# Attention, feed-forward and eight experts on one core: the first stage in a written order of single steps, with the first chunk's diagonal terms computed on TensorE

## The chip, the cores and the metric

One core of one Trainium2 chip runs the whole program in one launch. The metric is device microseconds (us) of the execution; each time is given as the median of several runs. The engines are named PE (TensorE), DVE (VectorE), ACT (ScalarE), POOL (GpSimd) and SP (SyncE, which here only issues DMAs).

## The reference

Three stages, each feeding the next, all in float32:

```
# 1. attention with a decaying state: B=2, H=8 heads, S=768 tokens, D=48
for t in range(S):
    cur = outer(u * k[t], v[t])                # the diagonal term, weighted by u
    y[t] = r[t] @ (state + cur)
    state = w[t][:, None] * state + outer(k[t], v[t])
# 2. feed-forward on x = y as 1536 tokens x 384
h = x @ w_in                                   # 384 x 2048
x = (h * clip(h + 3, 0, 6) / 6) @ w_out        # 2048 x 384
# 3. eight experts, all of them for every token, weighted by a Sinkhorn routing P
out = sum over e of P[:, e] * (relu(x @ w1[e]) @ w2[e])     # 384 x 1024 x 384
```

The weights of stage 2 come as 64-bit words and are made into float32 on the chip.

## The kernel before, in words

**Attention in chunks.** The tokens of each batch entry are cut into six chunks of 128; a *block* is one chunk of one of the two batch entries, twelve in all. A block loads its decays `w` (226 KB), `r` and `k` by dimension (`rk`, 448 KB), `v` by token (192 KB), and `r` and `k` once more by token (`rkt`, 384 KB). `prep0` (L149) makes running products of the decays by two scans on DVE, `prep1` multiplies them into `r` and `k`. `scores` (L188) multiplies `k` and `r` on PE and turns `k` over; `masks` (L203) copies the scores out on ACT and cuts the upper triangle on POOL; `outputs` (L215) multiplies by `v`, adds the part of the state, and sums `k` times `v` for the next state; `update` (L237) brings the state on. The diagonal term is apart: `diag0` (L173) multiplies `r`, `k` and `u` by token on POOL, `diag1` (L180) sums each head's 48 numbers on DVE and scales `v` by the sums in eight ACT steps, and `evac` (L232) adds the result to the output. `transposes` and `parts` (L250, L256) turn the block over and split it in a high and a low part, so that the feed-forward can multiply in reduced-width float32 three times (high-high, low-high, high-low) and keep the precision.

**Feed-forward in units.** A *unit* is one of 16 slices of 128 hidden columns for one chunk of both batch entries (256 columns): 96 units. `ff1_up` (L266) is nine matmuls of 128x256, a clamp step and a product (ACT L277, DVE L279), and a split (ACT L282, DVE L283). `ff1_down` (L286) is nine matmuls into two sums in PSUM, and comes two units later. Units are grouped in *cells*: a cell is a chunk and a range of slices, whose sum is copied out or added at its end (L298 to L304). Chunks 0 to 2 go through slices 0 to 5, then 6 to 11, then 12 to 15 (L753); chunks 3 to 5 through all sixteen at once.

**Weights.** Each pair of slices needs a half of `w_in` and a half of `w_out` (768 KB each as 64-bit words): `load_half` (L51) issues the load from SP into one of three buffers, `split_half` (L61) takes three DVE steps (L69 to L71), one ACT step and one DVE subtraction (L113, L114). There are 16 such halves.

**What sets the order.** Each engine and each DMA queue works off its own instructions in order, and waits at the head of its queue. The first block of code is written in an order by hand (L806 to L814), then units, attention stages and conversions are put at unit numbers (`at`, L761 to L800). That order is only a priority: up to the second unit of the experts a planner, which has its own costs for instructions, decides the order on each engine and queue. From there on (L871) the written order holds as it is.

Of the kernel before, what the change touches and what calls it, by code (L numbers as in the profile page):

```python
# [18 lines left out]
DM = H * D  # L19
# [23 lines left out]

class Kernel:
# [16 lines left out]
    def split_half(self, i, n, eng, after=None):  # L61
        if after is not None:
            with self.tc.issue_after(after.ins):
                return self.split_half(i, n, eng)
        nc = self.nc
        st = self.staged.pop((i, n)).rearrange("p (x t) -> p x t", t=2)
        low, high = st[:, :, 0], st[:, :, 1]
        x = self.tmp.tile([128, KT * CH], U32, tag="x", name="x")
        nc.vector.tensor_scalar(out=x, in0=high, scalar1=3, scalar2=0x3FFFFFF8, op0=ALU.logical_shift_left, op1=ALU.bitwise_and)  # L69
        nc.vector.scalar_tensor_tensor(out=x, in0=high, scalar=0xC0000000, in1=x, op0=ALU.bitwise_and, op1=ALU.bitwise_or)  # L70
        nc.vector.scalar_tensor_tensor(out=x, in0=low, scalar=29, in1=x, op0=ALU.logical_shift_right, op1=ALU.bitwise_or)  # L71
        if self.general:
            self.clamp_exponents(x, high)
        self.parts_of("ab"[n], x.bitcast(F32), (i // NCH, i % NCH, n), eng)
# [29 lines left out]
    def split_chunk(self, i, eng):  # L104
        st = self.staged.pop(i)
        h = KT * CH
        for n in range(2):
            self.parts_of("ab"[n], st[:, n * h:(n + 1) * h], (2 + i // NCH, i % NCH, n), eng)

    def parts_of(self, nm, x, key, eng):  # L110
        hi = self.wp.tile([128, KT * CH], F32R, tag=f"w{nm}h", name=f"w{nm}h")
        lo = self.wp.tile([128, KT * CH], F32R, tag=f"w{nm}l", name=f"w{nm}l")
        self.nc.scalar.activation(hi, x, AF.Copy)  # L113
        eng.tensor_tensor(out=lo, in0=x, in1=hi.bitcast(F32), op=ALU.subtract)  # L114
        self.wt[key] = hi, lo
# [9 lines left out]
    def att_load(self, c, b):  # L125
        nc, att = self.nc, self.att
        src = self.dm[b, c]
        w = att.tile([KR, WCOL], F32, tag="w", name="w")
        nc.sync.dma_start(out=w, in_=src[:, 2 * NP * C:])
        rk = att.tile([KR, 2 * NP * C], F32, tag="rk", name="rk")  # L130
        nc.sync.dma_start(out=rk, in_=src[:, :2 * NP * C])
        v = att.tile([C, DM], F32, tag="v", name="v")
        nc.sync.dma_start(out=v, in_=self.tm[b, c][:, 2 * DM:])
        self.loaded[c, b] = w, rk, v

    def att_load_tokens(self, c, b):
        self.tokens_of = c, b
        self.rkt = self.att.tile([C, 2 * DM], F32, tag="rkt", name="rkt")
        self.nc.sync.dma_start(out=self.rkt, in_=self.tm[b, c][:, :2 * DM])

    def att_stages(self, c, b):
        nc, att = self.nc, self.att
        w, rk, vt = self.loaded.pop((c, b))
        r = rk[:, :NP * C].rearrange("p (i t) -> p i t", i=NP)
        k = rk[:, NP * C:].rearrange("p (i t) -> p i t", i=NP)
        q = {}
        first, last = c == 0, c == NC - 1

        def prep0():  # L149
            wi = w[:, 1:].rearrange("p (i t) -> p i t", i=NP)[:, :, :C]  # L150
# [3 lines left out]
                data1=self.d1e.rearrange("p i t -> p (i t)"), initial=0.0, op0=ALU.mult, op1=ALU.add)  # L154
            rev = lambda x: x[:, ::-1]
            d1 = self.d1f
# [5 lines left out]
            q["f"], q["e"] = f, e  # L162

        def prep1():
            f, e = q["f"], q["e"]
            nc.vector.tensor_tensor(out=r, in0=r, in1=e[:, :, :C], op=ALU.mult)
            nc.vector.tensor_tensor(out=k, in0=k, in1=f[:, :, 1:], op=ALU.mult)
            if not last:
                pt = att.tile([KR, NP, 1], F32, tag="pt", name="pt")
                nc.vector.tensor_copy(pt, e[:, :, C:])  # L170
                q["pt"] = pt

        def diag0():  # L173
            assert self.tokens_of == (c, b)
            rt, kt = self.rkt[:, :DM], self.rkt[:, DM:]
            nc.gpsimd.tensor_tensor(out=rt, in0=rt, in1=kt, op=ALU.mult)
            nc.gpsimd.tensor_tensor(out=rt, in0=rt, in1=self.ubt, op=ALU.mult)
            q["z"] = rt

        def diag1():  # L180
            sd = att.tile([C, H], F32, tag="sd", name="sd")
            nc.vector.tensor_reduce(out=sd, in_=q["z"].rearrange("p (h d) -> p h d", h=H), axis=AX.X, op=ALU.add)
            dv = att.tile([C, DM], F32, tag="dv", name="dv")
            for h in range(H):
                nc.scalar.activation(dv[:, h * D:(h + 1) * D], vt[:, h * D:(h + 1) * D], AF.Copy, scale=sd[:, h:h + 1])  # L185
            q["dv"] = dv

        def scores():  # L188
            early = first and b == 1
            sc = [(self.psg if early else self.psa).tile([C, NP, C], F32, tag="g" if early else "sc", name="sc")  # L190
                  for _ in range(2)]
# [4 lines left out]
            if not last:  # L196
                kp = (self.psx if early else self.psa).tile([C, NP, KR], F32, tag="xa" if early else "m", name="kp")
                for i in range(NP):
                    nc.tensor.transpose(kp[:, i, :], k[:, i, :], self.ident[:KR, :KR])
                q["kp"] = kp  # L200
            q["sc"] = sc

        def masks():  # L203
            a = att.tile([C, 2, NP, C], F32, tag="a", name="a")
            for j in range(2):
                nc.scalar.activation(a[:, j], q["sc"][j], AF.Copy)
                nc.gpsimd.affine_select(out=a[:, j], in_=a[:, j], pattern=[[0, NP], [1, C]], compare_op=ALU.is_gt,
                                        fill=0.0, base=0, channel_multiplier=-1)
            q["a"] = a
            if not last:  # L210
                ks = att.tile([C, NP, KR], F32, tag="ks", name="ks")
                nc.scalar.activation(ks, q["kp"], AF.Copy)
                q["ks"] = ks

        def outputs():  # L215
# [10 lines left out]
            if not last:  # L226
                u = self.psa.tile([KR, NP, 2 * D], F32, tag="m", name="u")
                for i in range(NP):
                    nc.tensor.matmul(u[:, i, :], q["ks"][:, i, :], vt[:, i * 96:(i + 1) * 96], start=True, stop=True)
                q["u"] = u  # L230
# [6 lines left out]
        def update():  # L237
            if last:
                return
            for j in range(2):  # L240
# [3 lines left out]
                else:  # L244
                    nc.vector.tensor_tensor(out=self.state[b][p, :, e], in0=q["u"][p, :, e],
                                            in1=self.state[b][p, :, e], op=ALU.add)
            for i in range(NP):
# [8 lines left out]
        def parts():  # L256
            if b == 0:
                self.x1[c] = tuple(self.x1p.tile([128, KT, NB1], F32R, tag=f"x1{s}", name=f"x1{s}") for s in "hl")
            hi, lo = (t[:, :, b * C:(b + 1) * C] for t in self.x1[c])
            nc.scalar.activation(hi, q["xp"], AF.Copy)  # L260
            nc.vector.tensor_tensor(out=lo, in0=q["xp"], in1=hi.bitcast(F32), op=ALU.subtract)

        return [prep0, prep1, diag0, scores, diag1, masks, outputs, evac, update, transposes, parts]


    def ff1_up(self, c, f, start, stop):  # L266
        nc = self.nc
        ah, al = self.up_parts(f // 8, f % 8)
        xh, xl = self.x1[c]
        ph = self.psg.tile([128, 512], F32, tag="g", name="ph")[:, :NB1]  # L270
        n = 0
        for kt in range(KT):
            for wa, xa in ((ah, xh), (ah, xl), (al, xh)):
                nc.tensor.matmul(ph, wa[:, kt, :], xa[:, kt, :], start=n == 0, stop=n == 3 * KT - 1)  # L274
                n += 1
        t = self.p1.tile([128, NB1], F32, tag="t", name="t")
        nc.scalar.activation(t, ph, AF.Relu, bias=self.three)  # L277
        u = t
        self.last_u = nc.vector.scalar_tensor_tensor(out=u, in0=t, scalar=6.0, in1=ph, op0=ALU.min, op1=ALU.mult)  # L279
        gh = self.p1.tile([128, NB1], F32R, tag="gh", name="gh")  # L280
        gl = self.p1.tile([128, NB1], F32R, tag="gl", name="gl")
        nc.scalar.activation(gh, u, AF.Copy)  # L282
# [660 lines left out]
```

## Time and profile before

| | us |
|---|---|
| median of 3 runs | 1134.25 (1133.76 to 1135.38) |
| the profiled execution | 1133.67 |
| its span, first to last instruction | 1131.6 |
| PE busy | 1098.3 (97% of the span) |
| DVE busy | 621.1 (55%) |
| ACT busy | 331.4 (29%) |
| POOL busy | 63.1 (6%) |

The page draws the span in 40 slices of 28.3 us, each digit the busy share in tenths, PEclk the granted clock of TensorE in tenths of full speed:

```profile
PE   7789989999999999999999999999999999999997
PEld 6678989999997888888888888888888888788887
DVE  8699795545643543545465456455656655532331
ACT  3555554445631321221121122112112211211211
POOL 4443220000000000000000000000000000000000
PEclk7698999999999999999999999999999999999999
```

The numbers of the table are means over stages that differ. In the first six slices DVE and POOL are busy with the attention and the conversions, and PE is below 9 tenths in five of them; later PE is at 9 in almost every slice. The views below cut the span at 3.8 us (the first scan), 130 us, 175 us and 325.5 us (the first matmul of the experts).

### The profile page before, as it was taken

The page shows a single profiled execution, that of the slowest core. Times are in us where ns is not written, and L with a number is a line of the kernel's source. Part 1 is how long each engine was busy: PE and PEld are TensorE (multiplying, and loading weights), DVE is VectorE, ACT ScalarE, POOL GpSimd, SP SyncE. Part 2 cuts the span into 40 slices and gives each one's busy share as a digit, 9 for nine tenths or more (in the row PEclk, how much of TensorE's full clock was granted, in tenths as well). Part 3 has the DMA queues.
Part 4 walks back from the last instruction along what each step waited for, and adds up shares of the span by engine and source line. Part 5 has one row for each costly group of instructions (what it writes and reads, how often), then busy time and mean ns, then how long its engine had stood idle before and what let it go on. Part 6 is the DMA issues. An engine that isn't in the chain of part 4 may idle for free.

```text
span 1131.6 us, 14831 instructions
## 1 busy us (share of the span) xinstructions
PE 1098.3 (97%) x5956; PEld 949.0 (84%) x5956; DVE 621.1 (55%) x1217; ACT 331.4 (29%) x690; POOL 63.1 (6%) x57
## 2 busy tenths in 40 slices
PE   7789989999999999999999999999999999999997
PEld 6678989999997888888888888888888888788887
DVE  8699795545643543545465456455656655532331
ACT  3555554445631321221121122112112211211211
POOL 4443220000000000000000000000000000000000
PEclk7698999999999999999999999999999999999999
DMA  9456330000110004101311320132244234100001
GB/s 300 134 162 199 111 124 10 24 24 1 57 57 28 1 1 140 38 17 51 118 53 54 96 78 28 53 117 72 71 134 131 56 105 147 56 1 29 29 14 45
DMA packets 45469, 83.93 MB, mean 74 GB/s; under 512 B 3440, under 2 KB 27216, under 8 KB 45392
## 3 DMA queue, kind: packets, MB, share of 16 engines
q1 hardware_dynamic: 45392, 82.89, 23.3%
q8 instruction: 49, 0.80, 0.3%
q14 instruction: 28, 0.23, 0.1%
HBM read 80.47 MB, written 2.41 MB: 73 GB/s over the span
## 4 chain that ended last, share of the span: by engine, by line
PE 87%; DVE 7%; DMA 2%; ACT 1%; POOL 1%; issue 1%; SPq 0%; ACTq 0%; DVEq 0%; POOLq 0%
PE ph L406 35%; PE y L429 33%; PE ph L274 7%; PE xa L296 5%; PE xb L296 2%; PE y L427 1%; DMA rkt<-in_tm_dram 1%; DVE x L70 1%; PE y L223 1%; DVE x L71 1%; DMA v<-in_tm_dram 1%; DVE gl L283 1%; PE y L219 1%; DVE e L152 1%; ACT dv L185 1%
## 5 line engine op out<-in xcount | busy, mean ns | idle before, releaser
L411 DVE SCALAR_TENSOR_TENSOR hl<-ph,hh 128x512 fp32r<-128x512 f32 x192 | 132.4, 690 | 376.9 <-ACT hh L410 375.8
L410 ACT ACTIVATE hh<-ph 128x512 fp32r<-128x512 f32 x192 | 114.9, 598 | 611.0 <-PE ph L406 611.0
L406 PE MATMUL ph<-x2h,wah 128*128 128x512 f32 x576 | 226.3, 393 | 0.9 <-DVE off L561 0.9
L406 PE MATMUL ph<-x2h,wal 128*128 128x512 f32 x576 | 224.6, 390 | 0.0
L406 PE MATMUL ph<-x2l,wah 128*128 128x512 f32 x576 | 224.4, 390 | 0.0
L429 PE MATMUL y<-hl,wbh 128*128 128x512 f32 x552 | 215.0, 389 | 0.0
L429 PE MATMUL y<-hh,wbh 128*128 128x512 f32 x552 | 214.9, 389 | 0.0
L429 PE MATMUL y<-hh,wbl 128*128 128x512 f32 x552 | 214.9, 389 | 0.0
L406 PEld LDWEIGHTS ph<-x2h,wah 128*128 128x128 f32 x576 | 108.2, 188 | 23.2 <-DVE off L561 1.0
L406 PEld LDWEIGHTS ph<-x2h,wal 128*128 128x128 f32 x576 | 108.2, 188 | 22.9
L406 PEld LDWEIGHTS ph<-x2l,wah 128*128 128x128 f32 x576 | 108.3, 188 | 21.7
L429 PEld LDWEIGHTS y<-hh,wbl 128*128 128x128 f32 x552 | 103.7, 188 | 21.5
L429 PEld LDWEIGHTS y<-hl,wbh 128*128 128x128 f32 x552 | 103.7, 188 | 21.5
L429 PEld LDWEIGHTS y<-hh,wbh 128*128 128x128 f32 x552 | 103.7, 188 | 21.5
L274 PE MATMUL ph<-x1h,wah 128*128 128x256 f32 x288 | 85.6, 298 | 3.1 <-DVE t L279 3.0
L274 PE MATMUL ph<-x1h,wal 128*128 128x256 f32 x288 | 82.3, 287 | 1.7 <-DVE wal L114 1.7
L274 PE MATMUL ph<-x1l,wah 128*128 128x256 f32 x288 | 82.5, 287 | 0.0
L277 ACT ACTIVATE t<-ph,three 128x256 f32<-128x256 f32 x96 | 44.5, 470 | 66.0 <-PE ph L274 57.1
L279 DVE SCALAR_TENSOR_TENSOR t<-t,ph 128x256 f32<-128x256 f32 x96 | 39.5, 416 | 43.8 <-ACT t L277 43.6
L296 PE MATMUL xa<-gl,wbh 128*128 128x256 f32 x192 | 55.9, 291 | 5.5 <-DVE gl L283 5.5
L274 PEld LDWEIGHTS ph<-x1h,wah 128*128 128x128 f32 x288 | 56.2, 196 | 5.5 <-DVE t L279 4.5
L274 PEld LDWEIGHTS ph<-x1h,wal 128*128 128x128 f32 x288 | 55.9, 195 | 2.1 <-DVE wal L114 2.1
(140 smaller groups left out, 1419.4 us busy)
## 6 DMA issues: line engine op xcount, KB each, us to landing
stg<-in_w_dram SPq DMA_DIRECT2D x64, 384.0 KB, 5.0
stg<-in_w_in_dram SPq DMA_DIRECT2D x8, 768.0 KB, 6.5
stg<-in_w_out_dram SPq DMA_DIRECT2D x8, 768.0 KB, 4.6
pb<-pd SPq DMA_DIRECT2D x8, 768.0 KB, 4.2
seen<-in_w_in_dram SPq DMA_DIRECT2D x8, 768.0 KB, 4.7
seen<-in_w_out_dram SPq DMA_DIRECT2D x8, 768.0 KB, 4.6
rk<-in_dm_dram SPq DMA_DIRECT2D x12, 448.0 KB, 4.1
seen<-in_dm_dram SPq DMA_DIRECT2D x12, 448.0 KB, 4.0
```

The costliest lines, as they stand in the source:

```text
L70: nc.vector.scalar_tensor_tensor(out=x, in0=high, scalar=0xC0000000, in1=x, op0=ALU.bitwise_and, op1=ALU.bitwise_or)
L71: nc.vector.scalar_tensor_tensor(out=x, in0=low, scalar=29, in1=x, op0=ALU.logical_shift_right, op1=ALU.bitwise_or)
L152: nc.vector.tensor_tensor_scan(out=e.rearrange("p i t -> p (i t)"), data0=w[:, :WCOL - 1], data1=self.d1e.rearrange("p i t -> p (i t)"), i ...
L185: nc.scalar.activation(dv[:, h * D:(h + 1) * D], vt[:, h * D:(h + 1) * D], AF.Copy, scale=sd[:, h:h + 1])
L274: nc.tensor.matmul(ph, wa[:, kt, :], xa[:, kt, :], start=n == 0, stop=n == 3 * KT - 1)
L277: nc.scalar.activation(t, ph, AF.Relu, bias=self.three)
L279: self.last_u = nc.vector.scalar_tensor_tensor(out=u, in0=t, scalar=6.0, in1=ph, op0=ALU.min, op1=ALU.mult)
L296: nc.tensor.matmul(o, wb[:, kt * 128:(kt + 1) * 128], ga, start=start and n == 0 and kt != 1, stop=stop and n == 2, skip_group_check=True)
L406: nc.tensor.matmul(ph, wa[:, kt, :], xa[:, kt, sl], start=n == 0, stop=n == 3 * KT - 1)
L410: nc.scalar.activation(hh, ph, AF.Relu)
L411: nc.vector.scalar_tensor_tensor(out=hl, in0=ph, scalar=0.0, in1=hh.bitcast(F32), op0=ALU.max, op1=ALU.subtract)
L429: nc.tensor.matmul(y, wb[:, sl], ha, **go)
```

## The change

The planner is off from the start of the kernel. The stage functions are cut into single steps that have short names: a letter with chunk and batch for the attention (`E00` is the first scan of chunk 0, batch 0), a letter with half for the weights (`w20` loads, `W Q q h l` convert), and a prefix with a unit number for the feed-forward (`p` up-matmuls, `t g gh gl` the four steps behind them, `d` down-matmuls, `oa ob` the copy out or the add at a cell's end). `ORDER` is a list of 1070 such names up to the second unit of the experts, and the kernel issues them one after the other, so each engine's and SP's order is that of the list:

```diff
+CELLS = [(0, 0, 4), (1, 0, 4), (2, 0, 4), (0, 4, 10), (1, 4, 10), (2, 4, 10), (0, 10, 16), (1, 10, 16), (2, 10, 16), (3, 0, 16), (4, 0, 16), (5, 0, 16)]
+ORDER = """
+    I00 J00 O00 su w00 I01 E00 J01 F00 O01 w01 P00 G00 R00 K00 B00 w10 W00 E01 S00 D00 F01 V00 ubt I10 T00 v00 P01 G01
+    I11 M00 R01 B01 k00 N00 m00 K01 U00 i10 n00 D01 W01 V01 S01 Q00 v01 u00 q00 Y00 s00 E10 w11 M01 h00 T01 N01 J10
+    O10 y00 m01 l00 Z10 X00 k01 H00 U01 F10 n01 z10 L00 I20 u01 Y01 P10 s01 D10 R10 i11 V10 K10 J11 O11 y01 S10 v10
+    W10 E11 Z11 X01 M10 T10 F11 H01 m10 N10 k10 L01 I21 n10 R11 U10 P11 K11 z11 Y10 Q01 q01 D11 w20 h01 S11 J20 y10
+    i20 V11 l01 v11 p.0 O20 u10 W11 M11 X10 E20 t.0 T11 N11 s10 p.1 g.0 F20 H10 gh.0 t.1 m11 gl.0 I30 k11 n11 g.1 d.0
...
+    gl.6 w40 h21 d.4 y21 O31 u21 X21 l20 s21 d.5 l21 H21 p.7 L21 d.6 W30 t.7 W31 g.7 p.8 Q30 gh.7 p.9 gl.7 t.8 q30 d.7
+    t.9 g.8 w41 h30 g.9 p.10 Q31 oa.7 gh.8 ob.7 gh.9 gl.8 gl.9 d.8 t.10 l30 d.9 g.10 q31 gh.10 p.11 gl.10 w50 h31 W40
...
+    gl.29 d.28 l70 t.30 p.31 g.30 E30 gh.30 d.29 t.31 gl.30 g.31 p.32 oa.29 gh.31 ob.29 t.32 gl.31 d.30 g.32 D30 gh.32
...
+    gl.94 d.93 t.95 g.95 e.0 gh.95 gl.95 d.94 eh.0 el.0 e.1 d.95 eh.1 el.1 oa.95 ob.95
+"""
```

`I J O` load decays, `rk` and `v`; `i` loads `rkt`; `E F` scan, `R K` multiply, `P` keeps the last decay; `S T` scores and the turned `k`; `M N m n` copy and mask; `k U u s` are the state's steps; `Y` the output, `V v` the eight ACT steps (now four and four), `y X H L` the rest. In chunk 0, `G B D` take the place of `i Z z D`: the product of `r` and `k` by dimension, before the decays are multiplied in, goes to PE, which sums it over the dimensions with `u` as the other factor, and DVE copies 8 numbers a token out:

```diff
+        def diag_g():
+            rku = q["rku"] = att.tile([C, 2 * DM], F32, tag="rkt", name="rku")[:KR, :NP * C].rearrange("p (i t) -> p i t", i=NP)
+            nc.vector.tensor_tensor(out=rku, in0=r, in1=k, op=ALU.mult)
+
+        def diag_b():
+            sp = q["sp"] = self.psa.tile([C, H], F32, tag="m", name="sp")
+            for i in range(NP):
+                nc.tensor.matmul(sp[:, 2 * i:2 * i + 2], q["rku"][:, i, :], self.su[:, i, :], start=True, stop=True)
+
+        def diag_c():
+            q["sd"] = att.tile([C, H], F32, tag="sd", name="sd")
+            nc.vector.tensor_copy(q["sd"], q["sp"])
...
+        ops = dict(E=scan_e, F=scan_f, R=mul_r, K=mul_k, J=load_rk, O=load_v, V=diag_v(0), v=diag_v(H // 2), S=scores, M=m0, m=m1, N=n0, n=n1,
+                   Y=outputs, y=evac, X=transposes, H=part_h, L=part_l)
+        ops |= dict(G=diag_g, B=diag_b, D=diag_c) if first else dict(i=load_tokens, Z=diag_z, z=diag_u, D=diag_s)
+        if not last:
+            ops |= dict(P=keep_p, T=turn_k, k=keep_k, U=sums, u=update, s=decay)
...
+            top.enter_context(tc.manual_schedule())
...
+            self.su = att.tile([KR, NP, 2], F32, name="su")
...
+            nc.gpsimd.memset(self.su, 0.0)
...
+            def load_su():
+                for h in range(H):
+                    i, j = h // 2, h % 2
+                    nc.sync.dma_start(out=self.su[64 * j:64 * j + D, i, j:j + 1],
+                                      in_=self.ub[0:1, h * D:(h + 1) * D].rearrange("o d -> d o"))
...
+            for name in ORDER.split():
+                steps[name]()
```

In the first chunk the scores of batch 1 also use the attention's own PSUM buffers (before: those of the feed-forward). From the third unit of the experts on, the code and its order are as before.

## Rows read from the trace of the kernel before

**Rows 1.** Windows: length, then busy us (x instructions) PE, PEld, DVE, ACT, POOL; PEclk; DMA.

```profile
20.00:30.00 10.00, 8.58 (x46) 8.09 (x47) 9.94 (x14) 2.35 (x6) 3.18 (x2) 0.50 0.80 260
3.80:130.00 126.20, 105.52 (x753) 97.51 (x752) 115.03 (x179) 64.62 (x182) 52.46 (x40) 0.81 0.62 195
45.00:130.00 85.00, 73.18 (x556) 68.31 (x556) 82.43 (x133) 48.25 (x134) 34.64 (x26) 0.90 0.57 178
130.00:175.00 45.00, 41.24 (x345) 39.70 (x345) 34.09 (x65) 22.47 (x54) 6.71 (x4) 1.00 0.29 94
175.00:325.50 150.50, 150.01 (x1268) 147.73 (x1267) 77.07 (x167) 73.71 (x173) 2.44 (x4) 1.00 0.07 20
325.50:1131.60 806.10, 799.50 (x3589) 662.65 (x3587) 393.68 (x803) 169.32 (x282) 0.00 (x0) 1.00 0.20 64
```

**Rows 2.** One line: duration ns min/median/max, first and last start in us.

```profile
L406 PE MATMUL ph<-x2h,wah x576: 387/389/505, 325.6 to 1118.8; 128*128 128x512 f32 x192
```

**Rows 3.** Groups of instructions of PE, 175 to 325.5 us: count, busy us, mean ns.

```profile
L274 PE MATMUL ph<-x1h,wah 128*128 128x256 f32 x183 | 52.3, 286 | 0.5 <-DVE t L279 0.5
```

**Rows 4.** Timeline of PE, 208 to 210 us: start us, duration us, instruction.

```profile
208.29 0.99 PE L229 MATMUL u<-v,ks 128*112 128x96 f32 x8
...
209.38 0.28 PE L274 MATMUL ph<-x1h,wal 128*128 128x256 f32 x1
209.50 0.28 PE L274 MATMUL ph<-x1h,wah 128*128 128x256 f32 x1
```

**Rows 5.** Groups of instructions of VectorE, 0 to 130 us.

```profile
L159 DVE TENSOR_TENSOR_SCAN f<-w,d1f 112x516 f32<-112x516 f32 x10 | 14.1, 1406 | 0.1
L71 DVE SCALAR_TENSOR_TENSOR x<-stg,x 128x768 uint32<-128x768 uint32 x12 | 13.7, 1145 | 0.1
...
L166 DVE TENSOR_TENSOR rk<-rk,e 112x512 f32<-112x512 f32 x9 | 7.6, 841 | 0.0
...
L182 DVE TENSOR_REDUCE sd<-rkt 128x8 f32<-128x384 f32 x10 | 5.5, 546 | 7.4 <-POOL rkt L177 7.4
```

**Rows 6.** Timeline of all engines, 0 to 13.1 us.

```profile
0.81 0.40 SPq L129 DMA_DIRECT2D w<-in_dm_dram  x1
...
1.26 0.42 SPq L131 DMA_DIRECT2D rk<-in_dm_dram  x1
...
3.80 1.23 DVE L152 TENSOR_TENSOR_SCAN e<-w,d1e 112x516 f32<-112x516 f32 x1 [1.49 <-DMA w<-in_dm_dram]
4.08 0.49 SPq L139 DMA_DIRECT2D rkt<-in_tm_dram  x1
...
7.62 1.23 DVE L152 TENSOR_TENSOR_SCAN e<-w,d1e 112x516 f32<-112x516 f32 x1
...
12.10 1.79 POOL L176 TENSOR_TENSOR rkt<-rkt 128x384 f32<-128x384 f32 x1 [10.04 <-DMA rkt<-in_tm_dram]
...
13.07 1.63 DVE L71 SCALAR_TENSOR_TENSOR x<-stg,x 128x768 uint32<-128x768 uint32 x1
```

**Rows 7.** Timeline of VectorE, 49 to 59 us.

```profile
49.87 0.95 DVE L71 SCALAR_TENSOR_TENSOR x<-stg,x 128x768 uint32<-128x768 uint32 x1
...
54.11 0.95 DVE L114 TENSOR_TENSOR wal<-x,wah 128x768 fp32r<-128x768 f32 x1
54.97 0.68 DVE L166 TENSOR_TENSOR rk<-rk,e 112x512 f32<-112x512 f32 x1
```

**Rows 8.** DMA issues of the first 45 us: count, KB each, median us to landing.

```profile
stg<-in_w_in_dram SPq DMA_DIRECT2D x3, 768.0 KB, 7.9
...
w<-in_dm_dram SPq DMA_DIRECT2D x7, 226.2 KB, 4.9
...
stg<-in_w_out_dram SPq DMA_DIRECT2D x2, 768.0 KB, 9.1
```

**Rows 9.** DMA issues of the whole span, by the page.

```profile
stg<-in_w_out_dram SPq DMA_DIRECT2D x8, 768.0 KB, 4.6
...
rk<-in_dm_dram SPq DMA_DIRECT2D x12, 448.0 KB, 4.1
```

More of the change, by code (lines that the diff above doesn't have):

```diff
@@ L161, in prep0 @@
                 initial=0.0, op0=ALU.mult, op1=ALU.add)
[L162 to L175, printed above, removed]
+            q["f"] = f
@@ L176, in diag0, with diag_u, diag_s @@
             nc.gpsimd.tensor_tensor(out=rt, in0=rt, in1=kt, op=ALU.mult)
+        def diag_u():
+            rt, kt = q["z"]
             nc.gpsimd.tensor_tensor(out=rt, in0=rt, in1=self.ubt, op=ALU.mult)
-            q["z"] = rt
-        def diag1():
+        def diag_s():
             sd = att.tile([C, H], F32, tag="sd", name="sd")
[L182 to L186, printed above, removed]
+            nc.vector.tensor_reduce(out=sd, in_=q["z"][0].rearrange("p (h d) -> p h d", h=H), axis=AX.X, op=ALU.add)
+            q["sd"] = sd
@@ L188, in scores, with diag_v, go @@
+        def diag_v(n):
+            def go():
+                if n == 0:
+                    q["dv"] = att.tile([C, DM], F32, tag="dv", name="dv")
+                for h in range(n, n + H // 2):
+                    nc.scalar.activation(q["dv"][:, h * D:(h + 1) * D], vt[:, h * D:(h + 1) * D], AF.Copy,
+                                         scale=q["sd"][:, h:h + 1])
+            return go
         def scores():
-            early = first and b == 1
-            sc = [(self.psg if early else self.psa).tile([C, NP, C], F32, tag="g" if early else "sc", name="sc")
-                  for _ in range(2)]
+            sc = [self.psa.tile([C, NP, C], F32, tag="sc", name="sc") for _ in range(2)]
@@ L225, in outputs, with sums @@
             q["y"] = y
[L226 to L230, printed above, removed]
+        def sums():
+            u = self.psa.tile([KR, NP, 2 * D], F32, tag="m", name="u")
+            for i in range(NP):
+                nc.tensor.matmul(u[:, i, :], q["ks"][:, i, :], vt[:, i * 96:(i + 1) * 96], start=True, stop=True)
+            q["u"] = u
         def evac():
@@ L266, in ff1_up @@
-    def ff1_up(self, c, f, start, stop):
-        nc = self.nc
[L268 to L282, printed above, removed]
-        nc.vector.tensor_tensor(out=gl, in0=u, in1=gh.bitcast(F32), op=ALU.subtract)
-        self.g[c, f] = (gh, gl)
@@ L286, in ff1_down @@
[L286 to L298 removed]
+        (m0, n0), (m1, n1) = mask(0), mask(1)
@@ new lines, in ff1_down, with up_steps, mm, relu @@
+    def ff1_down(self, c, f, start, stop):
+        for step in self.down_steps(c, f, start, stop):
+            step()
+    def up_steps(self, c, f):
+        nc, q = self.nc, {}
+        def mm():
+            ah, al = self.up_parts(f // 8, f % 8)
+            xh, xl = self.x1[c]
+            ph = q["ph"] = self.psg.tile([128, 512], F32, tag="g", name="ph")[:, :NB1]
+            n = 0
+            for kt in range(KT):
+                for wa, xa in ((ah, xh), (ah, xl), (al, xh)):
+                    nc.tensor.matmul(ph, wa[:, kt, :], xa[:, kt, :], start=n == 0, stop=n == 3 * KT - 1)
+                    n += 1
+        def relu():
+            q["t"] = self.p1.tile([128, NB1], F32, tag="t", name="t")
+            nc.scalar.activation(q["t"], q["ph"], AF.Relu, bias=self.three)
+        def mul():
+            nc.vector.scalar_tensor_tensor(out=q["t"], in0=q["t"], scalar=6.0, in1=q["ph"], op0=ALU.min, op1=ALU.mult)
+        def upper():
+            q["gh"] = self.p1.tile([128, NB1], F32R, tag="gh", name="gh")
+            nc.scalar.activation(q["gh"], q["t"], AF.Copy)
+        def lower():
+            gl = self.p1.tile([128, NB1], F32R, tag="gl", name="gl")
+            nc.vector.tensor_tensor(out=gl, in0=q["t"], in1=q["gh"].bitcast(F32), op=ALU.subtract)
+            self.g[c, f] = (q["gh"], gl)
+        return mm, relu, mul, upper, lower
@@ new lines, in down_steps, with mm, first_a @@
+    def down_steps(self, c, f, start, stop):
+        nc = self.nc
+        def mm():
+            bh, bl = self.down_parts(f // 8, f % 8)
+            gh, gl = self.g.pop((c, f))
+            if start:
+                self.xa = self.psx.tile([128, 2, NB1], F32, tag="xa", name="xa")
+                self.xb = self.psx.tile([128, 1, NB1], F32, tag="xb", name="xb")
+            for kt in range(KT):
+                o = self.xa[:, kt, :] if kt < 2 else self.xb[:, 0, :]
+                for n, (wb, ga) in enumerate(((bh, gh), (bh, gl), (bl, gh))):
+                    nc.tensor.matmul(o, wb[:, kt * 128:(kt + 1) * 128], ga, start=start and n == 0 and kt != 1,
+                                     stop=stop and n == 2, skip_group_check=True)
+        def first_a():
@@ L306, in x2_parts, with more, out_a, out_b @@
+        def more(o, p):
+            nc.vector.scalar_tensor_tensor(out=o, in0=p, scalar=1.0 / 6.0, in1=o, op0=ALU.mult, op1=ALU.add)
+        done = self.begun
+        def out_a():
+            more(self.x2f[c][:, 0:2, :], self.xa) if c in done else first_a()
+        def out_b():
+            more(self.x2f[c][:, 2:3, :], self.xb) if c in done else first_b()
+        return (mm, out_a, out_b) if stop else (mm,)
     def x2_parts(self, c):
-        nc = self.nc
+        self.x2_upper(c)
+        self.x2_lower(c)
@@ L816, in last_block @@
+            steps = {}
             def last_block():
@@ L839, in fast, with begin, fill @@
-            at(n1 + LAG - 1, second)
+            def begin(c, b):
+                for s, fn in self.att_steps(c, b).items():
+                    steps[f"{s}{c}{b}"] = fn
+            def load_su():
[3 more added lines that the diff above has]
+                                      in_=self.ub[0:1, h * D:(h + 1) * D].rearrange("o d -> d o"))
+            def fill():
+                nc.tensor.matmul(wp, warm[:, :128], warm, start=True, stop=True)
@@ new lines, in fast @@
+            steps |= {"last": last_block, "hpool": hidden_pool, "su": load_su, "_": fill,
+                      "ubt": lambda: nc.sync.dma_start(out=self.ubt, in_=self.ub)}
+            for c in range(NC):
+                for b in range(B):
+                    steps[f"I{c}{b}"] = lambda c=c, b=b: begin(c, b)
+                steps[f"xh{c}"] = lambda c=c: self.x2_upper(c)
+                steps[f"xl{c}"] = lambda c=c: self.x2_lower(c)
+            for i in range(F1 // CH):
+                for n in range(2):
+                    steps[f"w{i}{n}"] = lambda i=i, n=n: self.load_half(i, n)
+                    for s, fn in zip("WQqhl", self.half_steps(i, n, nc.vector)):
+                        steps[f"{s}{i}{n}"] = fn
@@ new lines, in fast @@
+            for i in range(NCH):
+                steps[f"load{i}"] = lambda i=i: self.load_chunk(i)
+                for s, fn in zip(("sa", "sb", "sc", "se"), self.chunk_steps(i, nc.vector)):
+                    steps[f"{s}{i}"] = fn
+            for n, u in enumerate(units):
+                for s, fn in zip(("p", "t", "g", "gh", "gl"), self.up_steps(*u[:2])):
+                    steps[f"{s}.{n}"] = fn
+                for s, fn in zip(("d", "oa", "ob"), self.down_steps(*u)):
+                    steps[f"{s}.{n}"] = fn
```

371 lines of the change are left out of this document (192 added, 179 removed).

## The prediction

> **What bounds the kernel now.** The window view comes first, because an average hides the stages. From 325.5 us, where the first matmul of the experts starts [rows 2], to the end PE is busy 799.5 of 806.1 us at full clock; from 175 to 325.5 us 150.0 of 150.5 [rows 1]. The change leaves the order of the experts alone, so those 806.1 us stay, and the question is when the experts can start. Before 175 us PE is not the bound. From 3.8 (first scan) to 130 us VectorE is busy 115.0 of 126.2 us and PE's clock is 0.81; at 20 to 30 us, with few matmuls ready, it is 0.50, the lower of its two levels, 1.2 GHz [rows 1].
>
> How much of the 325.5 us is needed? Up to 175 us PE has started 35 of 96 up-products. From 175 us the rest are 1104 records of 256 columns at 118 ns, 130 us, and the attention of the last chunks, 20 us [rows 1, 3, 4]: the up-products are 3 x 183 of them. The same paces give 35 ups and 33 downs at 9 x 0.118 = 1.06 us, 72 us, and some 45 us of attention before 175 us: 117 of 175, so 58 us of PE are lost there. That is the most that any order can win back, and not all of it, since the first block's chain (load, scan, scores, mask, output) has to run first.
>
> VectorE spends this time badly in two ways. By 130 us it has scanned ten of twelve attention blocks though only six are wanted by the first 48 units [rows 5], so four blocks of about 5.8 us stand ahead of weight conversions that PE waits for. And its instructions are stretched while GpSimd runs: one third step of a conversion takes 1.63 us beside a 1.79 us GpSimd product, against 0.95 alone [rows 6, 7].
>
> **The change part by part.** *Paces.* On a full VectorE the next instruction starts 0.08 us before the last one's duration is over (0.95 us long, next start after 0.86) [rows 7]. So, from the shortest durations in that stretch [rows 5, 7]: a scan 1.14, reciprocal 0.09, each product with r or k 0.60, reduce, output and part 0.47 each, state update 0.72, decay copy 0.07. A block is 5.8 us. A converted half is 0.47 + 3 x 0.87 = 3.1 us, a unit's two steps 0.33 each. (Lines without a row here likewise.)
>
> *What contention costs.* The VectorE work of 3.8 to 130 us at these paces: 12 halves 37, ten pairs of scans 24, nine pairs of products 11, the rest of the attention 16, units 12: 100 us. Busy was 115.0 with 40 GpSimd instructions beside it [rows 1, 5], so 0.37 us an instruction.
>
> *The first chunk's diagonal.* It removes two loads of 384 KB, four GpSimd products and two reduces; it adds per block one product of 112x512 (0.60), four matmuls and a copy of 128x8 (0.1). VectorE: 2 x (0.7 - 0.47) = +0.5 us. The four matmuls have no row; a pair of chunk sums (8 records) takes 1.0 us at full clock [rows 4], so 0 to 2 us per block at half clock, on a PE that waits there anyway: 0 taken; without that cover up to 4. Four GpSimd instructions fewer: -1.5 us. The new constant is eight DMAs of 48 single elements, ahead of the first weights in SP's queue. SP issues one every 0.46 us [rows 6], so the first weight half and the second block's loads are issued 3.7 us later. Bounds: 0, if the stream of bytes is what they wait for, and 3.7.
>
> The Trainium skill (DMA: Bandwidth & Descriptors, Specifications) says that pieces under 512 B miss line rate because the engine reads, changes and writes; these are 4 B. No row has such a load. By the rule the eight would hold up the data behind them beyond their issue; if by as much again, 3.7 us, an estimate, the sum would be 1112.
>
> *The start in bytes.* 2884 KB (two blocks, one weight half, one token tile) had landed by 12.1 us, when the first GpSimd product started, and the first 226 KB by 3.8: 320 KB a us [rows 6, 8]. In the new order 1.6 MB stand ahead of the second block's decays, so they land at 8.9 us, or 10.6 with the 3.7 us gap, where its scan began at 7.6. Some 4.2 MB stand ahead of the third block's: 17 to 19 us, about when VectorE gets there. Then the token tile has one buffer, so its load, two products, mask and reduce follow one another: 0 to 2 us on the reduce of the third or fourth block. Together 1.5 to 6.5 us; I take 4.5, as the issue row says that the gap is real.
>
> *The written order.* I add VectorE's paces along the list and ask at each PE step when its input is done. The largest sum is much the same from unit 2 to unit 25, within 4 us, which means that the list keeps PE and VectorE level; I take down-product 8. Ahead of its input stand two first-chunk blocks (12.0), four others (23.1), six halves (18.5), four steps of the next two and a second 0.87 (3.5), 19 unit steps (6.3), two copies (0.7): 64.1 us. The blocks of chunks 3 to 5 come after unit 30. GpSimd's 22 instructions ahead of it cost 22 x 0.37 = 8.1 us.
> PE's work from there to the experts: 85 ups and 86 downs, 171 x 1.06 = 181; six blocks, about 5.8 us each and 4.5 without a state for the last two, and, as the 20 us above are a tenth more than their parts sum to, 35: 216.
> Start of the experts: 3.8 (first scan) + 64.1 + 8.1 + 4.5 (early stalls) + 2.6 (what VectorE idled in 45 to 130 us before [rows 1]; the list mixes its work as finely as the planner did) + 216 = 299 us, and 1 for PE's own gaps: 300.
>
> *Other cells.* As many cells, copies and adds as before; the first pass needs two weight pairs instead of three, and that is in the sum. *Single steps, no planner.* Same instructions; what they cost or save is their place. On SP the list puts each load behind the wait of the one before; its slack up to first use is 3.7 to 17 us of VectorE pace, for landings of about 4.1 us [rows 9]. Only the fourth block's r and k (3.7) and those of the last blocks (1 to 2.5, where PE has work in hand) are short: 0 to 2 us, inside the early stalls.
>
> So 325.5 - 300 = 25.5 us. Against this execution's 1133.67 us (2.1 over its span of 1131.6) that is 1108.2; the median, 1134.25, stands 0.6 above, so 1108 to 1109. Bounds: early stalls of 1.5 and contention halved give 1101, with no idle either 1098; early stalls of 6.5 and three times the idle 1115.
>
> **The rivals.**
> *A, the forecast: VectorE paces the front until unit 25, then PE.* 1108; its own range is 1100 to 1115. Chance 0.55.
> *B, PE's clock falls back.* PE and VectorE are level, so short waits recur. For: in 45 to 130 us, PE busy 73 of 85 us, the clock was 0.90, that is 17 us at the lower level and 8.5 us of work lost [rows 1]. Against: from 130 us, busy 41 of 45, it was 1.00 [rows 1]. Over the 120 us between the first unit and unit 40 the same share loses 12: 1120. Chance 0.20.
> *C, near PE's floor.* Half the early stalls, half the contention and no idle: 1098 to 1100. For: the order also draws GpSimd's work apart. Against: stalls on both sides add up when two engines are level. Chance 0.14.
> *D, GpSimd blocks VectorE outright.* Each of the 22 instructions would hold it for as long as it lasts, 52.5 / 40 = 1.31 us on the mean [rows 1], instead of 0.37: +21, 1129. For: the third step's mean of 1.145 us against 0.95 [rows 5, 7]. Against: those 52.5 us cost VectorE 15, and the reduces were not stretched at all [rows 5]. Chance 0.04. The Trainium skill (SBUF — State Buffer, Who interferes with whom) states such a rule: a VectorE instruction with two SBUF inputs and a GpSimd one that reads SBUF exclude each other for the whole instruction. The step of 1.63 us agrees with it, the sum of 15 us doesn't.
> *E, slower: loads exposed in SP's queue.* The planner spread the loads; the list issues them just before use. The second weight halves of the first 45 us landed in 9.1 us instead of the kernel's usual 4 to 5 [rows 8, 9]. At some ten loads the slack is under 7.2 us: r and k of blocks 4, 5 and 6, the token tiles, four weight halves. If they land late at each, and every stall of VectorE goes to PE as there is no slack, 10 x 3.5 = 35 us: 1143. It decides from 2.6 us a load. For: those 9.1 us. Against: the DMA engines were 0.8 busy at 20 to 30 us; later 0.3 to 0.6 [rows 1]. Chance 0.07.
>
> **How the numbers follow.** A 0.55, B 0.20, C 0.14, D 0.04, E 0.07. Faster by over 0.2% (2.3 us, about what a measurement of this kernel can tell from no change): all of A, B, C and D but 0.01, so 0.92; within 0.2%, 0.02, from the passage between B and E; slower 0.06, the most of E. Range: the lower end of C less a little, 1096, to 1124, a little above B; D, E and the tails of B and C stay out.
>
> **What would show it.** The first expert matmul at about 300 us; the first up-product near 35; VectorE over 0.93 busy from 35 to 130 us; twelve or more units started by 85 us; no fourth-chunk scan before 110 us; the same 806 us after the experts start. The forecast is wrong if PE is idle over 15 us between 40 and 160 us, if its clock is below 0.9 there (B), or if VectorE waits mainly for DMA (E).

## The result, and the profile after

| | before | after | forecast |
|---|---|---|---|
| median, us | 1134.72 (4 runs) | 1114.57 (1114.29 to 1114.74, 4 runs) | 1108 (1096 to 1124) |
| ratio to before | 1 | 0.9823 (95% interval 0.9806 to 0.984) | |
| span of the profiled execution | 1131.6 | 1112.7 | |
| first expert matmul | 325.6 | 305.9 | 300 |
| first up-product | 38.6 | 44.8 | near 35 |
| end of the split steps of units 8 and 9 | 100.5 | 89.5 | 83.1 (unit 8) |

The change won 20 us of the 26 forecast. The starts of the experts and of the first up-product are read from one line each (duration ns min/median/max, first and last start); the first answers to [rows 2]:

```profile
L575 PE MATMUL ph<-x2h,wah x576: 387/389/504, 305.9 to 1099.0; 128*128 128x512 f32 x192
...
L406 PE MATMUL ph<-x1h,wah x288: 278/279/580, 44.8 to 304.5; 128*128 128x256 f32 x144
```

The windows answer to [rows 1], with the same columns. 3.80 us is the first scan, 44.75 the first up-product, 305.90 the first expert matmul, and 89.52 the end of the split steps of units 8 and 9, which come right behind each other (unit 8's ends at 89.2). Where nothing else is said, "unit 8" below means the end of this pair:

```profile
20.00:30.00 10.00, 9.86 (x59) 8.88 (x57) 7.12 (x13) 4.96 (x13) 3.21 (x4) 0.60 0.62 191
3.80:89.52 85.72, 75.84 (x536) 69.72 (x535) 72.68 (x120) 45.08 (x127) 25.67 (x22) 0.80 0.64 189
44.75:130.00 85.25, 81.92 (x665) 79.28 (x664) 80.40 (x142) 48.41 (x118) 14.43 (x12) 0.96 0.49 147
130.00:175.00 45.00, 43.75 (x389) 42.49 (x388) 42.58 (x75) 25.78 (x74) 15.97 (x15) 0.96 0.32 90
305.90:1112.70 806.80, 799.35 (x3588) 662.28 (x3586) 393.65 (x803) 169.30 (x282) 0.00 (x0) 1.00 0.20 64
```

The same stretch of the kernel before, up to its end of this pair:

```profile
3.80:100.53 96.73, 78.43 (x552) 72.03 (x551) 86.80 (x135) 48.09 (x139) 39.12 (x31) 0.79 0.65 205
```

The experts start 19.7 us earlier. 11.0 of these are won up to this pair, where VectorE was busy 86.8 us before and 72.7 now, and 8.7 behind it (225.1 us from there to the experts before, 216.4 now). From the experts' start on nothing changed: 806.8 us here, 806.1 before. From 44.75 to 130 us PE and VectorE are level: busy 81.9 and 80.4 of 85.25 us. The whole miss lies ahead of 89.5 us, where VectorE was busy 72.7 us (0.3 of them for unit 9), as forecast (64.1 + 8.1 = 72.2), and idle 13.0, forecast 7.1. The waits of VectorE from 3.8 to 89.52 us (total, times, longest) say for what:

```profile
DVE ys L348 <- PE y L336: 5.0, 2, 2.7
DVE x L124 <- DMA stg<-in_w_in_dram: 2.8, 1, 2.8
DVE e L237 <- DMA w<-in_dm_dram: 1.9, 2, 1.5
DVE t L414 <- ACT t L411: 1.6, 3, 0.9
DVE sd L287 <- POOL rkt L283: 0.9, 1, 0.9
DVE rk L253 <- DMA rk<-in_dm_dram: 0.5, 1, 0.5
```

The largest is a wait for PE, an engine for which the forecast took no stall there; the three waits for DMA come to as much together, 5.2 us, but for these it had a term. PE's timeline (start, duration, idle before and its releaser) and clock show how PE came to be late. In the windows of 2 us the clock is the third number from the right:

```profile
10.91 0.60 PE L310 MATMUL kp<-ident,rk 112*128 112x112 f32 x4
15.73 1.84 PE L270 MATMUL sp<-su,rku 112*128 112x2 f32 x8 [4.21 <-DVE rku L265]
17.43 1.79 PE L343 MATMUL u<-v,ks 128*112 128x96 f32 x8
...
21.16 3.65 PE L336 MATMUL y<-v,a 128*128 128x48 f32 x16
```

```profile
12.00:14.00 2.00, 0.00 (x0) 0.00 (x0) 1.75 (x4) 0.46 (x2) 0.00 (x0) 1.00 1.01 286
14.00:16.00 2.00, 0.27 (x2) 0.30 (x2) 1.97 (x4) 2.00 (x9) 0.00 (x1) 0.58 1.03 395
16.00:18.00 2.00, 2.00 (x11) 2.00 (x11) 1.67 (x4) 0.96 (x3) 1.74 (x2) 0.50 1.06 386
18.00:20.00 2.00, 2.00 (x15) 1.83 (x16) 1.84 (x4) 1.79 (x8) 0.00 (x0) 0.50 1.08 279
22.00:24.00 2.00, 2.00 (x12) 2.00 (x11) 0.18 (x1) 1.07 (x2) 2.00 (x3) 0.50 0.94 255
```

PE waits 4.21 us for the second block's `rku`; behind this wait the clock is at the lower level, and 8 records of `sp` take 1.84 us where the first block's took 0.95. PE then works without a gap and yet late; `y` is done at 24.8 us, and VectorE is busy 0.18 of the 2 us before.

### The profile page after: what moved, and what is told of

Same layout as the page of the kernel before. It is cut to its first block, busy times and chain, and to the rows that moved or that the text cites. A ratio compares the mean times of both kernels' runs of the same rounds, so it can differ in the third digit from the quotient of the medians.

```text
span 1112.7 us, 14865 instructions
## 1 busy us (share of the span) xinstructions
PE 1091.7 (98%) x5972; PEld 945.4 (85%) x5972; DVE 618.8 (56%) x1219; ACT 330.5 (30%) x690; POOL 49.8 (4%) x54
## 4 chain that ended last, share of the span: by engine, by line
PE 90%; DVE 5%; DMA 2%; ACT 1%; issue 1%; POOL 0%; SPq 0%; DVEq 0%; ACTq 0%; POOLq 0%
PE ph L575 35%; PE y L605 34%; PE ph L406 8%; PE xa L439 5%; PE xb L439 3%; PE y L603 1%; PE y L336 1%; DMA w<-in_dm_dram 1%; DMA v<-in_tm_dram 1%; DVE x L132 1%; DVE x L128 1%; PE sc L303 1%; DVE e L237 1%; DVE gl L422 1%; PE y L332 1%
## 5 line engine op out<-in xcount | busy, mean ns | idle before, releaser
L406 PE MATMUL ph<-x1h,wah 128*128 128x256 f32 x288 | 82.7, 287 | 1.6 <-ACT wah L194 1.6
L439 PE MATMUL xa<-gh,wbh 128*128 128x256 f32 x192 | 55.9, 291 | 0.0
```

Source lines behind the costliest of these rows:

```text
L439: nc.tensor.matmul(o, wb[:, kt * 128:(kt + 1) * 128], ga, start=start and n == 0 and kt != 1, stop=stop and n == 2, skip_group_check=True)
```

## The experiments

All ratios are to the kernel before, measured in the same session, in brackets the 95% interval; the changed kernel's is 0.9823 [0.9806, 0.984]. All edits are to the changed kernel.

**1. Is it the clock?** `_` in the list is one matmul on constants of no use, already there and unused.

```diff
-    ... I10 T00 v00 P01 ...
+    ... I10 T00 _ (38 times) v00 P01 ...
```

> Theory (clock): the forecast's missing 6 us are VectorE's 5.0 us of waits for two y products that PE computes at 1.2 GHz, and PE's clock fell behind its wait of 4.2 us at 11.5 us. 38 small bf16 matmuls on data of no use fill that wait, so the granted clock stays at 1.00 after 14 us, the 12 us of PE work between 15.7 and 28 us take 6, the first y wait (2.66 us) goes, the first up-product comes at 41 to 42 us instead of 44.75 and the median is 1111 to 1112. Rival (start): PE is only late because loads and the eight small DMAs made the blocks late; then the clock may be full and the time stays within 1 us of 1114.6. Rival (clock not won): with small f32 matmuls the clock falls anyway, 0.5 to 0.6 from 16 to 28 us, and nothing changes.

1113.75 us, 0.9818 [0.9802, 0.9833]: no gain that can be told. The clock stayed at 1.00 through the gap, but fell at the next one (0.66 from 20 to 30 us); unit 8 ended 0.9 us earlier, the experts began at 306.1. Holding the clock in one gap isn't enough.

The second kernel adds `_` six times behind each of U00 S01 Y00 T01 X00 U01 Y01 S10 X01 T10 U10.

> The same 38, and six more fillers behind each of eleven PE steps up to the first up-product (104 in all, some 7 us of PE at full clock). Theory (clock): the granted clock is near 1.00 from 4 to 50 us, both y waits (2.66 and 2.33 us) go, the first up-product comes at 40 us, the median is 1109 to 1110. Rival (start): within 1 us of 1114.6. Rival (fillers in the way): where PE is the late engine the fillers lengthen its chain by up to 7 us, 1115 to 1118.

1111.18 us (1108.06 to 1113.18), 0.9798 [0.9782, 0.9814]. Both `y` waits are gone, unit 8 ends at 83.6 us and the experts begin at 301.6. The clock at 20 to 30 us is 1.00:

```profile
20.00:30.00 10.00, 8.80 (x81) 7.79 (x81) 8.81 (x14) 5.79 (x19) 4.81 (x4) 1.00 0.70 203
```

Up to there VectorE waits nowhere for PE, so the 104 fillers stand in nobody's way, and the clock theory holds in the trace. The medians of this and the changed kernel differ by 3.4 us, with intervals that just overlap, so the time alone doesn't settle it yet.

**2. Is it the start?** First the place of su's eight DMAs: `su` moved from ahead of `w00` to behind `J01`.

> The eight 4-byte-piece DMAs of the constant stand behind the first weight half and the second block's loads instead of ahead of them. If their issue (3.9 us of SP) is what made the second block late, its first scan starts near 9 us instead of 12.21, PE's wait of 4.2 us at 11.5 us shrinks to about 1, and the median falls by 2 to 3.5 us to 1111 to 1112.5. If the stream of bytes sets it, the scan moves by under 1 us and the time by under 0.5. By the clock theory a shorter wait could also leave the clock at 1.00, which would add the first y wait: 1109 to 1110.

1115.45 us, 0.9825 [0.981, 0.9839]: nothing won. SP's queue says why (start, duration of the issues); the first fence is of the changed kernel, the second of this one:

```profile
2.19 3.93 SPq L945 DMA_DIRECT2D su<-in_ub_dram  x8
```

```profile
3.67 8.40 SPq L943 DMA_DIRECT2D su<-in_ub_dram  x8
12.12 0.43 SPq L227 DMA_DIRECT2D v<-in_tm_dram  x1
```

Behind the large loads the same eight issues take 8.40 us instead of 3.93, PE then waits 3.5 us for `su`, and everything behind them in the queue is late. So the same bytes in fewer DMAs:

```diff
-                for h in range(H):
-                    i, j = h // 2, h % 2
-                    nc.sync.dma_start(out=self.su[64 * j:64 * j + D, i, j:j + 1],
-                                      in_=self.ub[0:1, h * D:(h + 1) * D].rearrange("o d -> d o"))
+                src = self.ub[0, :].rearrange("(i j d) -> d i j", j=2, d=D)
+                for j in range(2):
+                    nc.sync.dma_start(out=self.su[64 * j:64 * j + D, :, j], in_=src[:, :, j])
```

> The constant su comes by two DMAs instead of eight (one for each half of the partitions, the same 384 pieces of 4 bytes). In the run with su behind the other loads its eight DMAs took 8.4 us of SP's queue instead of 3.9, so their place was not the question, their issue is. If the issue holds the first block back, SP is free 3 us earlier, the second block's first scan starts at 9 to 10 us instead of 12.21, and the median falls by 2 to 3 us, to 1111.5 to 1112.5. If the stream of bytes (DMA share 1.0 from 10 to 20 us) sets that scan, it moves by under 1 us and the time by under 0.5. If 4-byte pieces cost by the piece and not by the issue, two DMAs hold SP as long as eight did and nothing moves.

1113.09 us (1110.88 to 1114.23), 0.9798 [0.9785, 0.9812]. The issue fell to 0.92 us and the second block's scan came at 10.42 instead of 12.21 us:

```profile
2.19 0.92 SPq L943 DMA_DIRECT2D su<-in_ub_dram  x2
```

Unit 8 ended 1.8 us earlier, but in the profiled execution the experts began at 305.8, as PE still ran at the lower clock (0.67 from 20 to 30 us) and lost it again. Alone it is worth 1.5 us by the medians and 2.8 by the ratios, with intervals that overlap.

> All 104 fillers and the two DMAs for su. If clock and start are two separate parts of the missing 6 us, the gains add: 1111.2 less 2 to 3, 1108 to 1109, with no y wait on VectorE, the clock at 1.00 from 4 to 58 us and the first expert matmul near 300 us. If the earlier start only moves the wait to the next load, it stays at 1111.

Both edits together: 1107.83 us (1106.57 to 1108.41), 0.9756 [0.9743, 0.977], faster than the changed kernel and than either edit alone, with intervals apart from all three. It differs from the kernel with two DMAs for su only in the fillers, and both were measured in one session: 5.3 us, the clear measure of what the fillers bring. The gains more than add (6.7 us together, 3.4 and 1.5 alone):

```profile
3.80:83.99 80.19, 76.17 (x640) 70.45 (x639) 72.14 (x120) 45.17 (x127) 26.42 (x22) 0.94 0.67 201
```

```profile
L575 PE MATMUL ph<-x2h,wah x576: 387/389/504, 300.6 to 1093.7; 128*128 128x512 f32 x192
```

The same 72 us of VectorE work, idle 8.1 us instead of 13.0, unit 8 at 84.0 and the experts at 300.6: most of the 6 us is found, and the forecast's own numbers come out once PE has its clock for most of the front and su comes by two DMAs. Two parts of the expectation failed: the clock still fell, to 0.63 from 44 to 58 us, and 1.8 us of waits for `y` are left. This is the fastest version of the study.

**3. GpSimd's order.** `Z11` moved to behind `n10`.

> GpSimd's first token product of block (1,1) stands behind the two masks of block (1,0) instead of ahead of them, so the masks start near 33.6 instead of 35.2 us. If GpSimd's order is what makes the second y product late, VectorE's second wait (2.33 us) falls to below 1 and the median by 1 to 1.5 us, to 1113 to 1113.5, unless the reduce of block (1,1), whose token product is now 3 us later, waits instead (then no change). By the clock theory the y product still takes 4.4 us at the lower clock and under half of the wait goes: 1114 to 1114.5.

1114.25 us, 0.9826 [0.9813, 0.984]; unit 8 ends at 89.5 as in the changed kernel, and VectorE waits 5.2 us for `y`. The masks start at 35.0 us instead of 35.2 and not at 33.6, as they wait for ACT's copy. The wait of 2.33 us falls to 1.40, and a new one of 1.11 comes ahead of it. GpSimd's order alone gains nothing.

**4. More of the same.** fill_su with 27 fillers in the gap, 34 more up to the first down-product, and `J11` ahead of `i11`.

> The run fill_su with three repairs that its trace points to: 27 instead of 38 fillers in the first gap (there they held PE 1.3 us past the point where the second block's product was ready), 34 more behind the steps between the first up-product and the first down-product (the clock fell at 44.8 us behind a gap there), and the load of block (1,1)'s r and k ahead of its token load (VectorE waited 1.6 us for it). If each wait goes to the end as the doses did, 2 to 4 us under 1107.8: 1104 to 1106, the clock at 1.00 to 60 us. If PE and VectorE are level by then, or the fillers come late, it stays at 1107 to 1108.

1108.87 us (1108.37 to 1111.99), 0.9789 [0.9775, 0.9804]: not better. The profiled execution has the clock at 0.98 up to unit 8 and the same ends (83.9 and 300.5), so the clock was no longer the limit. VectorE idles 5.5 us there instead of 8.1, but is busy 74.6 instead of 72.1, and the one eats up the other. Why it is busy longer, and why the other executions are slower, is open.

**5. Does VectorE pace?** Seven extra VectorE instructions, `x`, behind gl.1 to gl.7:

```diff
+            def dose():
+                nc.vector.scalar_tensor_tensor(out=scr, in0=scr, scalar=0xC0000000, in1=scr,
+                                               op0=ALU.bitwise_and, op1=ALU.bitwise_or)
...
-    ... gl.1 ... gl.2 ...
+    ... gl.1 x ... gl.2 x ...
```

> Seven extra VectorE instructions on data of no use (128x768, 0.87 us of pace each: 6.1 us), one behind each of the split steps of units 1 to 7, between some 52 and 87 us. If VectorE paces the front there, as the forecast has it, all of it goes to the end: 1120 to 1121. If PE paces from the first up-product on (it is busy 81.9 of 85.3 us from 44.75 to 130), the doses fall into VectorE's 4.9 us of idle time there and cost 0 to 2.5 us: 1114.5 to 1117. A lower clock after longer PE waits would add up to 2 us.

1121.24 us, 0.988 [0.9865, 0.9895]: 6.7 us more than the changed kernel, for seven instructions of 0.95 us (one of 1.74, beside GpSimd):

```profile
L953 DVE SCALAR_TENSOR_TENSOR scr<-scr x7: 945/951/1743, 52.5 to 92.0; 128x768 uint32<-128x768 uint32 x7
```

Unit 8 ended 6.8 us later, the experts began at 313.1, 7.2 later. The clock is 0.92 from 44.75 to 130 us instead of 0.96; but up to unit 8 VectorE is busy 6.2 us more and idle only 0.7 more, so it is the added work that counts. Work of VectorE goes to the end in full, though PE is busy 96% there. Then the same behind gl.14 to gl.20:

> The seven extra VectorE instructions (6.1 us of pace) behind the split steps of units 14 to 20, between some 103 and 123 us. By the forecast (VectorE paces until unit 25, the sums level within 4 us) 4 to 6 us go to the end: 1118.5 to 1120.5. If PE paces from unit 8 on and VectorE has run ahead by then, 0 to 2: 1114.5 to 1116.5.

1119.58 us, 0.987 [0.9854, 0.9885]: 5.0 us more. VectorE still paces there, and some 1 us of the 6.1 finds room.

**6. What brought the gain?** The planner on again, with the same list as priorities:

```diff
         with ExitStack() as top:
-            top.enter_context(tc.manual_schedule())
             self.pools(top)
...
+            top.enter_context(tc.manual_schedule())
             for n in range(LAG, len(units) + LAG):
```

> The same list, cells and diagonal on PE, but the planner is on again up to the third unit of the experts, so the list gives priorities only. If the held order brings the gain, the planner starts later blocks ahead of conversions again (a scan of the fourth chunk before 110 us, fewer than 25 units by 130 us) and the median is 1122 to 1132. If the gain comes from the sequence alone, as priorities, from the cells or from the diagonal, the median is within 2 us of 1114.6.

1140.72 us, 1.0052 [1.0035, 1.007]: slower than before, 26 us slower than the changed kernel, and above the 1122 to 1132 expected. Its window from the first scan to the end of unit 10's split step (unit 8's alone ends at 122.4 us, with VectorE busy 112.9 us up to there):

```profile
3.80:125.10 121.30, 89.09 (x613) 82.22 (x612) 113.99 (x174) 58.01 (x157) 45.52 (x32) 0.72 0.69 212
```

VectorE is fuller than in the changed kernel (94% of this stretch, there 85% up to unit 8), and it does some 113 us of work ahead of unit 8 instead of 72. Its groups from 3.8 to 130 us (count | busy, mean ns) show which, and under them those of the changed kernel:

```profile
L245 DVE TENSOR_TENSOR_SCAN f<-w,d1f 112x516 f32<-112x516 f32 x9 | 13.1, 1451 | 0.0
...
L420 DVE TENSOR_TENSOR gl<-t,gh 128x256 fp32r<-128x256 f32 x12 | 6.0, 512 | 0.7 <-ACT gh L416 0.5
```

```profile
L132 DVE SCALAR_TENSOR_TENSOR x<-stg,x 128x768 uint32<-128x768 uint32 x15 | 15.7, 1049 | 0.2
...
L422 DVE TENSOR_TENSOR gl<-t,gh 128x256 fp32r<-128x256 f32 x28 | 13.2, 476 | 1.0 <-ACT gh L418 0.9
...
L247 DVE TENSOR_TENSOR_SCAN f<-w,d1f 112x516 f32<-112x516 f32 x6 | 7.4, 1238 | 0.2
```

The planner scans nine blocks where the held list scans six, and has 12 units where it has 28 (before: ten and 17, [rows 5] for the scans). Without the held order nothing of the gain is left: the same list as priorities, the cells and the diagonal bring none of it under the planner.

Next, the first chunk's diagonal by token loads again, in the held list (`su B00 B01 G00 G01` out; `i00 Z00 z00 i01 Z01 z01` in; the loads `ubt` and `i10` move to fit):

> The list held as written, but the first chunk's diagonal computed as before the change (token loads of 384 KB, two GpSimd products and a reduce for each of its two blocks; no su, no product on PE). Forecast's sum: VectorE 0.5 us less, GpSimd's four instructions 1.5 us more, the eight small DMAs (3.7 us of issue) gone, the token loads' bytes (768 KB at 320 KB a us, 2.4 us) and their chain through the one token buffer added: 0 to 3 us slower, 1114.5 to 1117.5. Rival: the diagonal on PE brings nothing and its small DMAs cost more than the tokens, 1112 to 1114. Other rival: without it the first chunk's output is late and much of the 20 us is lost, over 1122.

1117.34 us (1115.06 to 1119.38), 0.9851 [0.9835, 0.9866]: 2.8 us slower in the median, with intervals that overlap. VectorE waits 5.9 us for the second block's token products and still 3.5 us for `y`, and the clock is 0.50 from 14 to 50 us:

```profile
DVE sd L285 <- POOL rkt L281: 5.9, 1, 5.9
DVE ys L346 <- PE y L334: 3.5, 2, 2.3
```

```profile
14.00:50.00 36.00, 29.29 (x153) 27.06 (x154) 25.72 (x40) 16.38 (x52) 16.16 (x13) 0.50 0.63 189
```

So the lower clock and the late `y` don't come from the new products on PE alone: without them they are there too.

Last, the cells of before in the held list, with the third weight pair's steps in one piece ahead of `p.4` and `d.4`, and chunks 2 to 5 four units later:

> The list held as written with the cells of before ((0,6), (6,12), (12,16) for chunks 0 to 2): the third weight pair is converted ahead of units 4 and 6, and the attention of chunks 2 to 5 stands four units later; VectorE's and PE's work is the same. The forecast's sums (VectorE's work ahead of a split step plus PE's work behind it, largest over the units) come to within 0.5 us of each other in the two lists, so 1113 to 1116. If the smaller first cells bring gain by themselves (PE has 12 units from two weight pairs), it is 1118 to 1122.

1143.57 us, 1.0079 [1.0065, 1.0093]: 29 us slower, where every theory had 1113 to 1122. VectorE's work to unit 8 (here unit 8 alone) is again 72.0 us, but it takes 101.6:

```profile
60.00:90.00 30.00, 15.37 (x94) 14.05 (x94) 19.03 (x29) 8.71 (x22) 0.63 (x1) 0.73 0.40 128
...
3.80:105.36 101.56, 78.16 (x510) 72.06 (x508) 72.04 (x113) 42.97 (x120) 23.36 (x22) 0.73 0.51 153
```

```profile
PE ph L404 <- ACT wah L192: 7.2, 1, 7.2
PE xa L437 <- ACT wbh L192: 6.0, 1, 6.0
```

With a conversion's five steps in one piece, VectorE and ACT hand it to and fro, and PE's next product, ready in nothing but this weight, holds all that stands behind it (its waits at 60 to 90 us, above). These two waits are 13 of the 16 us by which unit 8 is late. Another 14 us are lost between unit 8 and the experts (at 335.9 us), where PE waits 7.3 us for VectorE's products of later blocks; the rest of these is not explained. So this run tells of a coarse list, not of the cells: what those are worth by themselves stays open. In the kernel before they weren't tried alone: with its blocks where they are, units 4 and 8 would come before their input.

## Why the prediction was right, and where it missed

- **The unit in which it was counted held.** VectorE's work ahead of unit 8: 72.2 forecast, 72.7 measured (72.3 without unit 9). PE's work from there to the experts: 216 forecast, 305.9 - 89.5 = 216.4. The rest: 806 and 806.8. The doses show that the first term is the path, and not only a number that fits.
- **Contention: right.** 72.7 - 64.1 = 8.6 us for 22 GpSimd instructions, 0.39 each, forecast 0.37. Rival D, as it was priced, is out: the 22 instructions were busy 25.7 us, and had they held VectorE for their whole length, it would have been busy up to 89.8. But this doesn't speak against the Trainium skill's rule (SBUF — State Buffer, Who interferes with whom), as the forecast took it: some 8 of the 25.7 us are GpSimd's own lengthening (at the shortest durations of its instructions they would be 17.5), and so are some 20 of the 52.5 us of the kernel before, by which the forecast judged it. So each side waits for the other, and the sums don't refute the rule. This stretch agrees with it: a GpSimd product that takes 1.00 us at the shortest takes 3.07 while VectorE's instructions on SBUF follow one another, and then VectorE's next one, with two SBUF inputs, takes 1.64 instead of 0.95:

```profile
65.41 3.07 POOL L283 TENSOR_TENSOR rkt<-rkt,ubt 128x384 f32<-128x384 f32 x1
...
66.67 0.94 DVE L128 SCALAR_TENSOR_TENSOR x<-stg,x 128x768 uint32<-128x768 uint32 x1
67.65 1.64 DVE L132 SCALAR_TENSOR_TENSOR x<-stg,x 128x768 uint32<-128x768 uint32 x1
```

- **"4.5 (early stalls) + 2.6 (idle)": the mis-sized term.** 13.0 instead of 7.1. By the list of waits, loads and tokens cost 6.1 us (2.8 + 1.9 + 0.5 + 0.9) instead of 4.5, inside the forecast's 1.5 to 6.5; ACT 1.9 instead of 2.6; and PE 5.3, 5.0 of it for `y`, for which nothing stood in the sum. The step that failed is this nothing: the early stalls were put together from loads and tokens, as if PE had time to spare in the first blocks, although the forecast had itself read the clock there, 0.50 at 20 to 30 us. "On a PE that waits there anyway: 0 taken" holds for the new products by themselves: VectorE waits 0.3 us for them, and without them the clock is no better and `y` still late (the run with token loads, diag_tokens). But PE's wait of 4.2 us leaves it at the lower clock, and so `y` is late twice. Rival B had the mechanism and put it behind the first unit; there, from 44.75 to 130 us, the clock was 0.96, and it fell ahead of it (0.67 from 3.8 to 44.75 us).
- **su: 0 to 3.7 us forecast; the gap is real.** The forecast had the second block's decays in at 10.6 us with the gap; the scan that waits for them started at 12.2, and at 10.4 with two DMAs. The number of issues counts; its price alone is small. Whether the small pieces themselves hold up the data behind them, as the forecast read the Trainium skill's rule (DMA: Bandwidth & Descriptors, Specifications), the runs can't tell, as all that load `su` have the same 384 pieces.
- **The diagonal: +0.5 to VectorE and little else forecast;** the run without it is 2.8 us slower, with overlapping intervals, by a stall of 5.9 us for tokens; its expectation, from the same terms, was 0 to 3.
- **The signs to look for.** Right: no fourth-chunk scan before 110 us (133.6), the same 806 us, PE idle 4 us from 40 to 160 at a clock of 0.94. VectorE's waits were not mainly for DMA, but nearly: 5.2 us up to unit 8, for PE 5.3. Wrong, all by the late start: the first up-product, some nine units started by 85 us instead of twelve, VectorE 0.91 busy from 35 to 130 us instead of over 0.93.
- **What the sum can't tell:** old_cells has the same sums and is 29 us slower. The forecast's "the list mixes its work as finely as the planner did" was no detail but a condition.

## What to carry to other kernels

Where two engines are level, add the pacing engine's work ahead of one unit to the other's work behind it; a few extra instructions at one place show which engine paces, and how far such a sum can be trusted. It holds only for a fine mix: look for steps put in one piece. In a start-up stage, ask of each engine's waits not only whether they are covered but at what clock PE comes out of them; idle matmuls on constants are cheap cover where PE would wait.

## What the runs showed that was not expected

- PE's clock stayed at 0.50 from 16 to 24 us with PE busy the whole time by the profile (2.00 of every 2 us shown above), after one wait of 4.2 us. With 104 fillers among the same products it was 1.00.
- Eight DMAs of 192 bytes cost SP 3.93 us of issue behind 0.9 MB of larger loads and 8.40 behind 2.3 MB, 0.49 and 1.05 us each.
